# Attention, then two gated layers: in the third pair of heads, where six operand moves stand in the transfer queue

## The chip, the cores and the metric

The kernel runs on one core of a Trainium2 chip. The metric is the device time of one execution in microseconds (us); the time before is the median of three runs. The engines run side by side, each through its own queue in order: TensorE (PE; its weight loads are PEld), VectorE (DVE), ScalarE (ACT), GpSimd (POOL) and SyncE (SP), which issues the DMA transfers.

## The reference

```python
mask = q_assign[:, :, :, None] == k_assign[:, :, None, :]
scores = scale * np.matmul(q, k.transpose(0, 1, 3, 2))
scores = np.where(mask, scores, -1000000000.0)
attn = np.exp(scores - np.max(scores, axis=-1, keepdims=True))
attn = attn / (np.sum(attn, axis=-1, keepdims=True) + 1e-09)
out = np.matmul(attn, v)
...
h = (x @ w1) * (x @ w2) @ w3 @ w_out
gate = 1.0 / (1.0 + np.exp(-(h @ w_gate)))
y = (gate * (h @ w_val)) @ w_out2
```

Two batches of 8 heads, 768 tokens, 64 columns a head. A query sees only the keys whose nearest of 16 centroids is the same as its own. The attention output goes through the two layers of 512 to 1024 and 512 to 1536 columns.

## The kernel before

The attention stage takes the first 236 us or so. Two heads of 64 rows lie side by side on the 128 partitions as a pair; there are 8 pairs, numbered from 0, so the third pair is pair 2. A pair has six blocks of 256 queries, three for each head; the loop runs over blocks i, with `pr, at = divmod(i, 6)`. The order of all instructions is written out by hand, and each engine works through its own in that order.

Numbers are kept as a high part and a low part, and a product is made of parts. For a head four operand tiles are needed: QH and KH hold the high parts of q and k (64 rows) and below them 16 rows of the mask; QX and KX hold high and low parts (128 rows). `scores(j)` multiplies them into a score tile s (128 queries by 768 keys), DVE takes the maximum (L342), ACT the exponentials (L353), PE transposes them (L363, tile pt), ACT and DVE split them (tiles ph and pl, L381 and L392; in some blocks ACT copies to pc and POOL splits), and PE multiplies with v into av (L404, L405). ACT copies av to xa (L413), which frees the one av buffer for the next block.

While a pair is computed, the next pairs are made ready:
- `prep_split(later)` splits the raw q and k of the pair after the next into tiles hi and lo (L192 on ACT, L194 on DVE for q; L56 on ACT and L59 on POOL for k). It begins in block `at == 3`. Tiles hi and lo have two buffers each, one for q and one for k, so a pair's hi overwrites that of the pair before it.
- `prep_scatter(pr, e)` moves the rows of head e from hi and lo into its operand tiles: six transfers of 192 KB, four of high parts and two of low parts. `operands` has three buffers for each operand tile. For head 0 they stand at the end of the pair before (`at == 5`); for head 1 of pairs 3 to 7 in block `at == 1`.
- `prep_mask(pr, e)` moves the mask rows of a head (tile ohT, made by DVE in L273, half of it changed by POOL in L292) into QH and KH: four transfers of 24 KB. It stands in block `at == 3` for both heads.

For pair 2 alone, `prep_scatter(2, 1)` stands in block `at == 3` of pair 1, between the masks of the two heads. The same block issues, on ACT behind the exponentials, the first `prep_split` of pair 3 (L192).

All these transfers go through SP's queue, in order. When a transfer's source isn't made yet or its target is still read, SP waits and everything behind it waits too.

Of the kernel before, what the change touches and what calls it, by code (L numbers as in the profile page):

```python
# [27 lines left out]
def tile_cluster_attention__then__moe__then__gated_moe(  # L28
# [32 lines left out]
    def move(dst, src):  # L61
        nc.sync.dma_start(dst.bitcast(F32), src.bitcast(F32))
# [109 lines left out]
    def load_v(pr, e=None):  # L172
        if e != 1:
            raw[pr, "v"] = core.tile([128, 2, KT, D], F32, tag="vraw", name=f"vraw{pr}", bufs=1)
        which = slice(0, 2) if e is None else slice(e, e + 1)
        nc.sync.dma_start(raw[pr, "v"][:, which], v[pr][:, which])


    opnd = {}
# [33 lines left out]
    def operands(pr, e):  # L213
        opnd[pr, e] = tuple(core.tile([rows, S], F32R, tag=tag, name=f"{tag}{pr}_{e}", bufs=3) for tag, rows in (("QH", 96), ("KH", 96), ("QX", 128), ("KX", 128)))
        return opnd[pr, e]
# [2 lines left out]
        nc.vector.scalar_tensor_tensor(out=lo, in0=x, scalar=0.125, in1=hi.bitcast(F32), op0=ALU.mult, op1=ALU.subtract)  # L218

    def prep_scatter(pr, e):  # L220
        qh, ql, kh, kl = opnd[pr, "hl"]
        r = slice(64 * e, 64 * e + 64)
        QH, KH, QX, KX = operands(pr, e)
        move(QH[0:64], qh[r])
        move(KH[0:64], kh[r])
        move(QX[0:64], qh[r])
        move(KX[64:128], kh[r])
        move(KX[0:64], kl[r])
        move(QX[64:128], ql[r])

# [45 lines left out]
    def prep_mask(pr, e):  # L276
        ohT = opnd[pr, "oh"]
        QH, KH, _, _ = opnd[pr, e]
        halves = [slice(HALF * h, HALF * h + HALF) for h in range(2)]
        if pr == 0 and e == 0:  # L280
            for h in range(2):
                nc.vector.tensor_scalar(out=KH[64:96, halves[h]], in0=ohT[64 + 32 * h : 96 + 32 * h], scalar1=-1.0, scalar2=BIG, op0=ALU.add, op1=ALU.mult)
                nc.scalar.copy(QH[64:96, halves[h]], ohT[32 * h : 32 * h + 32])
            return
        if pr == 0:
            for h in range(2):
                nc.scalar.activation(KH[64:96, halves[h]], ohT[64 + 32 * h : 96 + 32 * h], AF.Copy, scale=BIG, bias=-BIG)
            nc.scalar.copy(QH[64:96, halves[0]], ohT[0:32])
            move(QH[64:96, halves[1]], ohT[32:64])
            return  # L290
        if e == 0:
            nc.gpsimd.tensor_scalar(out=ohT[64:128], in0=ohT[64:128], scalar1=-1.0, scalar2=BIG, op0=ALU.add, op1=ALU.mult)  # L292
        for h in range(2):
            at = 32 * h + C * e
            move(QH[64 : 64 + C, halves[h]], ohT[at : at + C])
            move(KH[64 : 64 + C, halves[h]], ohT[64 + at : 64 + at + C])
# [87 lines left out]
    def split_lo(i, k2):  # L384
        if (i, k2) not in pts:
            return
        src = pts.pop((i, k2))
        ph, pl = phs[i, k2]
        if by_pool(i, k2):
            split(src, ph, pl, nc.gpsimd, nc.gpsimd)  # L390
        else:
            nc.vector.tensor_tensor(out=pl, in0=src, in1=ph, op=ALU.subtract)  # L392
# [128 lines left out]
    hl = [core.tile([128, S], F32R, tag=tag, name=f"{tag}0_{w}", bufs=2) for w in range(2) for tag in ("hi", "lo")]  # L521
    opnd[0, "hl"] = hl
    QH, KH, QX, KX = operands(0, 0)
# [26 lines left out]
    scaled_lo(hl[1][up], q[up], hl[0][up])  # L550
    nc.gpsimd.tensor_tensor(out=hl[3][up], in0=k[up], in1=hl[2][up], op=ALU.subtract)
    prep_scatter(0, 1)
    load_v(0, 1)
    prep_v(0, 0)
# [15 lines left out]
    if True:  # L570
        for i in range(-2, NB + 2):
            pr, at = divmod(i, 6)
            nxt = pr + 1 if 0 <= i and pr + 1 < NPR else None
# [23 lines left out]
                join_x(pr - 1, 1)  # L597
            if nxt and nxt > 1 and at == 1:
                load_v(nxt)
                if nxt > 2:  # L600
                    prep_scatter(nxt, 1)
            if nxt and at == 3:
                for e in range(2):
                    if nxt == e == 1:
                        prep_scatter(1, 1)
                    prep_mask(nxt, e)
                    if nxt == 2 and e == 0:
                        prep_scatter(2, 1)
            split_lo(i - 1, 2)
            split_hi(i, 0)  # L610
            split_lo(i, 0)
# [190 lines left out]
    for n, (m, u) in enumerate(order):  # L802
# [6 lines left out]
        if n in W34_AT:  # L809
# [4 lines left out]
            for half in range(2):  # L814
                hl = wo_pool.tile([128, 2, HK, 128], F32R, tag="w3", name=f"w3_{j}_{half}", bufs=3)
# [437 lines left out]
```

## Time and profile before

| | us |
|---|---|
| median of 3 runs | 758.09 (757.73 to 758.61) |
| the profiled execution | 756.68 |
| its span in the trace | 754.7 |
| PE busy | 742.6 (98% of the span) |
| DVE busy | 575.6 (76%) |
| ACT busy | 473.5 (63%) |
| POOL busy | 414.7 (55%) |

The profiled execution took 1.98 us more than its span, and 1.41 us less than the median. Of the chain that ended last, 92% is work of PE. In the line of 40 slices PE is at 9 tenths or more nearly everywhere; the mean granted clock is 0.998 of full speed.

### The profile page before, as it was taken

How to read it: one execution, taken by the hardware profiler on the slowest of the kernel's cores; microseconds unless marked ns; L12 is line 12 of the kernel's file. 1: busy time of each engine (PE TensorE's matmuls, PEld its weight loads, DVE VectorE, ACT ScalarE, POOL GpSimd, SP SyncE). 2: the span in 40 equal slices, each digit the busy share in tenths (PEclk: the TensorE clock that was granted, in tenths of full speed). 3: DMA queues.
4: the chain of work that ended last, by engine and by line, in shares of the span. 5: the costliest groups of instructions: out<-in, count | busy, mean ns of one | idle time of the engine just before them, and what ended most of it. 6: DMA issues, size and time to landing. Idle time of an engine off the chain costs nothing.

```text
span 754.7 us, 12290 instructions
## 1 busy us (share of the span) xinstructions
PE 742.6 (98%) x4270; PEld 672.2 (89%) x4270; DVE 575.6 (76%) x893; ACT 473.5 (63%) x994; POOL 414.7 (55%) x420
## 2 busy tenths in 40 slices
PE   8997999999999999999999999999999999999998
PEld 7886988998998888888888999999999999999996
DVE  7996989999987777766753387686687978869675
ACT  8986888988886456555542355776756454565630
POOL 4776787888682665433231036675547646375510
PEclk9999999999999999999999999999999999999999
DMA  6675666785533444434340001221303113030004
GB/s 194 179 184 141 178 155 173 184 208 140 139 94 112 140 134 146 137 115 140 112 140 1 1 1 56 85 84 56 113 0 106 63 56 112 18 122 29 29 0 168
DMA packets 29054, 80.10 MB, mean 106 GB/s; under 512 B 5056, under 2 KB 6656, under 8 KB 28992
## 3 DMA queue, kind: packets, MB, share of 16 engines
q1 hardware_dynamic: 28992, 79.32, 36.0%
q8 instruction: 34, 0.56, 0.3%
q14 instruction: 28, 0.23, 0.1%
HBM read 52.46 MB, written 3.19 MB: 74 GB/s over the span
## 4 chain that ended last, share of the span: by engine, by line
PE 92%; DVE 2%; ACT 2%; DMA 1%; issue 1%; POOL 1%; SPq 0%; DVEq 0%; ACTq 0%; POOLq 0%
PE p L67 13%; PE p L66 13%; PE p L65 13%; PE s L330 8%; PE pt L363 7%; PE p_a L66 4%; PE p_a L67 4%; PE p_a L65 4%; PE av L404 4%; PE av L405 4%; PE p_b L65 2%; PE p_b L66 2%; PE p_b L67 2%; PE w34p L67 2%; PE w34p L66 2%; PE w34p L65 2%
## 5 line engine op out<-in xcount | busy, mean ns | idle before, releaser
L342 DVE TENSOR_REDUCE nm<-s 128x1 f32<-128x768 f32 x96 | 90.8, 947 | 7.9 <-PE s L330 6.6
L353 ACT ACTIVATE e<-s,nm 128x768 f32<-128x768 f32 x96 | 88.2, 919 | 13.1 <-DVE nm L342 12.6
L404 PE MATMUL av<-ph,vx 128*128 128x256 f32 x288 | 81.8, 310 | 5.0 <-ACT xa L413 4.7
L363 PE MATMUL pt<-ident,e 128*128 128x128 f32 x576 | 86.3, 273 | 0.2 <-DVE sm L246 0.2
L392 DVE TENSOR_TENSOR pl<-pt,ph 128x512 fp32r<-128x512 f32 x113 | 75.7, 682 | 10.9 <-ACT ph L381 9.7
L67 PE MATMUL p<-x,w 128*128 128x512 f32 (+1 forms) x208 | 80.2, 385 | 0.0
L66 PE MATMUL p<-x,w 128*128 128x512 f32 (+1 forms) x208 | 80.1, 385 | 0.0
L65 PE MATMUL p<-x,w 128*128 128x512 f32 (+1 forms) x208 | 80.1, 385 | 0.0
L405 PE MATMUL av<-pl,vx 128*128 128x256 f32 x288 | 75.6, 290 | 0.6 <-DMA raw<-in_qkT_dram 0.2
L116 POOL TENSOR_TENSOR w_a<-w_f 128x512 uint32<-128x512 uint32 x30 | 32.1, 1070 | 76.2 <-DVE w_f L115 36.1
L381 ACT CAST ph<-pt 128x512 fp32r<-128x512 f32 x113 | 64.7, 591 | 14.7 <-PE pt L363 13.4
L363 PEld LDWEIGHTS pt<-ident,e 128*128 128x128 f32 x576 | 68.1, 142 | 4.6 <-DVE sm L246 0.5
L1132 DVE TENSOR_TENSOR acc<-p,acc 128x512 f32<-128x512 f32 x59 | 40.5, 687 | 29.3 <-PE p L67 29.2
L948 POOL TENSOR_TENSOR wgv_a<-wgv_f 128x512 uint32<-128x512 uint32 x24 | 25.3, 1054 | 66.6 <-DVE wgv_f L947 38.3
L1026 ACT COPY s<-p_a 128x384 f32<-128x384 f32 x72 | 34.5, 479 | 43.1 <-PE p_a L67 42.8
L404 PEld LDWEIGHTS av<-ph,vx 128*128 128x128 f32 x288 | 54.9, 191 | 7.1 <-ACT xa L413 5.5
L405 PEld LDWEIGHTS av<-pl,vx 128*128 128x128 f32 x288 | 55.2, 192 | 3.3 <-DVE pl L392 3.2
L67 PE MATMUL p<-wo,u 128*128 128x512 f32 (+1 forms) x146 | 57.3, 393 | 0.0
L66 PE MATMUL p<-wo,u 128*128 128x512 f32 (+1 forms) x146 | 57.1, 391 | 0.0
L330 PE MATMUL s<-KH,QH 80*128 80x512 f32 x192 | 54.9, 368 | 1.7 <-ACT e L353 0.8
L65 PE MATMUL p<-wo,u 128*128 128x512 f32 (+1 forms) x146 | 56.3, 386 | 0.0
L330 PE MATMUL s<-KX,QX 128*128 128x512 f32 x192 | 49.9, 342 | 0.0
(254 smaller groups left out, 2222.9 us busy)
## 6 DMA issues: line engine op xcount, KB each, us to landing
wgv_f<-in_w_gv_dram SPq DMA_DIRECT2D x24, 512.0 KB, 3.3
wo_f<-in_w_out_dram SPq DMA_DIRECT2D x20, 512.0 KB, 3.2
w_f<-in_w_dram SPq DMA_DIRECT2D x16, 512.0 KB, 3.5
w_f<-in_w3T_dram SPq DMA_DIRECT2D x16, 512.0 KB, 3.3
raw<-in_qkT_dram SPq DMA_DIRECT2D x16, 384.0 KB, 4.7
r<-r_dram SPq DMA_DIRECT2D x16, 192.0 KB, 3.8
xb<-xa SPq DMA_DIRECT2D x15, 192.0 KB, 3.5
out_dram<-acc SPq DMA_DIRECT2D x11, 256.0 KB, 2.0
```

What stands on the lines that cost most here:

```text
L65: nc.tensor.matmul(ps, whi, xhi, start=start, stop=False, skip_group_check=more)
L66: nc.tensor.matmul(ps, whi, xlo, start=False, stop=False, skip_group_check=more)
L67: nc.tensor.matmul(ps, wlo, xhi, start=False, stop=stop, skip_group_check=more)
L330: nc.tensor.matmul(sp[:, c], products[n][0], products[n][1][:, c], start=n == 0, stop=n == 1)
L342: nc.vector.tensor_reduce(out=nms[j], in_=sps[j][:, 0:S], axis=AX.X, op=ALU.max, negate=True)
L353: nc.scalar.activation(et, sps.pop(j)[:, 0:S], AF.Exp, bias=nms.pop(j), accum_out=acc_x[pr, "sum"][:, at : at + 1])
L363: nc.tensor.transpose(pt[:, kk, 128 * t : 128 * t + 128], exps[2 * i + t][:, k0 : k0 + 128], ident)
L381: nc.scalar.copy(ph, pt)
L392: nc.vector.tensor_tensor(out=pl, in0=src, in1=ph, op=ALU.subtract)
L404: nc.tensor.matmul(avs[i], w, ph[:, kk, :], start=kt == 0, stop=False)
L405: nc.tensor.matmul(avs[i], w, pl[:, kk, :], start=False, stop=kt == KT - 1)
L1132: nc.vector.tensor_tensor(out=acc[:, t, :], in0=bk, in1=acc[:, t, :], op=ALU.add)
```

## The change

`prep_scatter` is divided into its four moves of high parts and its two moves of low parts. For the second head of pair 2, the four moves of high parts now stand in block `at == 1` of pair 1, directly behind the load of v. The two moves of low parts stay in block `at == 3`, between the masks of the two heads. Nothing is added or left out.

```diff
     def prep_scatter(pr, e):
+        prep_scatter_hi(pr, e)
+        prep_scatter_lo(pr, e)
+
+    def prep_scatter_hi(pr, e):
         qh, ql, kh, kl = opnd[pr, "hl"]
...
         move(KX[64:128], kh[r])
+
+    def prep_scatter_lo(pr, e):
+        qh, ql, kh, kl = opnd[pr, "hl"]
+        r = slice(64 * e, 64 * e + 64)
+        QH, KH, QX, KX = opnd[pr, e]
         move(KX[0:64], kl[r])
         move(QX[64:128], ql[r])
...
                 load_v(nxt)
+                prep_scatter_hi(nxt, 1)
                 if nxt > 2:
-                    prep_scatter(nxt, 1)
+                    prep_scatter_lo(nxt, 1)
...
                     if nxt == 2 and e == 0:
-                        prep_scatter(2, 1)
+                        prep_scatter_lo(2, 1)
```

The queue of SP in pair 1, from the load of v (vraw) on; QH_0 and KH_0 belong to the first head of pair 2, the names with _1 to its second head. Before:

```order
L176 DMA vraw_830<-in_v_dram 128x768
L62 DMA QH_0_690<-ohT_None 16x384
L62 DMA KH_0_691<-ohT_None 16x384
L62 DMA QH_0_690<-ohT_None 16x384
L62 DMA KH_0_691<-ohT_None 16x384
L62 DMA QH_1_969<-hi_0_546 64x768
L62 DMA KH_1_970<-hi_1_617 64x768
L62 DMA QX_1_971<-hi_0_546 64x768
L62 DMA KX_1_972<-hi_1_617 64x768
L62 DMA KX_1_972<-lo_1_618 64x768
L62 DMA QX_1_971<-lo_0_547 64x768
L62 DMA QH_1_969<-ohT_None 16x384
```

And in the changed kernel:

```order
L176 DMA vraw_830<-in_v_dram 128x768
L62 DMA QH_1_832<-hi_0_546 64x768
L62 DMA KH_1_833<-hi_1_617 64x768
L62 DMA QX_1_834<-hi_0_546 64x768
L62 DMA KX_1_835<-hi_1_617 64x768
L62 DMA QH_0_690<-ohT_None 16x384
L62 DMA KH_0_691<-ohT_None 16x384
L62 DMA QH_0_690<-ohT_None 16x384
L62 DMA KH_0_691<-ohT_None 16x384
L62 DMA KX_1_835<-lo_1_618 64x768
L62 DMA QX_1_834<-lo_0_547 64x768
L62 DMA QH_1_832<-ohT_None 16x384
```

The four moves out of hi have passed the four masks of the first head; the two moves out of lo have the masks ahead of them as before, and four transfers fewer between.

On ACT no row moved. This is its queue in block `at == 3` of pair 1 and the next, before and after alike but for line numbers: the split of pair 3 (hi_0_994), and what stands behind it.

```order
L353 ACTIVATE e_992,ss_656<-s_949,nm_962 128x768
L192 ACTIVATE hi_0_994<-raw_0_756 128x768
L381 CAST ph_1_1018<-pt_1_1013 128x512
L413 COPY xa_0_875<-av 128x256
L353 ACTIVATE e_1034,ss_656<-s_1005,nm_1031 128x768
L381 CAST ph_2_1041<-pt_2_1025 128x512
L378 COPY pc_1054<-pt_0_1044 128x512
```

The split stands ahead of the copy of av to xa and of the next exponentials.

## Rows read from the trace of the kernel before

**Rows 1.** PE's waits over the whole span: total us, times, longest.
```profile
PE av L404 <- ACT xa L413: 4.7, 1, 4.7
```

**Rows 2.** Timeline of ACT, pair 1: start, duration, instruction, [idle before, releaser].
```profile
59.49 0.91 ACT L353 ACTIVATE e<-s,nm 128x768 f32<-128x768 f32 x1
...
65.52 0.84 ACT L192 ACTIVATE hi<-raw 128x768 fp32r<-128x768 f32 x1 [5.04 <-DMA QX<-hi]
```

**Rows 3.** Timeline of PE, pair 1, same columns.
```profile
61.87 0.60 PE L363 MATMUL pt<-ident,e 128*128 128x128 f32 x4
67.16 0.49 PE L404 MATMUL av<-ph,vx 128*128 128x256 f32 x1 [4.69 <-ACT xa L413]
...
70.81 0.36 PE L404 MATMUL av<-ph,vx 128*128 128x256 f32 x1
...
75.58 0.27 PE L438 MATMUL s<-ident,ss 128*12 128x128 f32 x1
```

**Rows 4.** Windows: busy us by engine, then PEclk, DMA share and GB/s.
```profile
52.50:56.50 4.00, 4.00 (x31) 3.68 (x30) 3.90 (x7) 3.08 (x7) 3.74 (x5) 1.00 0.55 147
...
62.50:66.50 4.00, 0.00 (x0) 0.00 (x0) 0.00 (x0) 0.98 (x2) 0.00 (x0) 1.00 0.97 210
66.50:70.50 4.00, 3.34 (x14) 3.15 (x15) 3.55 (x5) 3.97 (x10) 1.37 (x2) 0.60 0.49 127
```

**Rows 5.** Timeline of SP's queue, pair 1: start and duration of each issue.
```profile
52.75 0.74 SPq L176 DMA_DIRECT2D vraw<-in_v_dram  x1
58.04 0.54 SPq L62 DMA_DIRECT2D QH<-ohT_None  x1
...
60.32 0.57 SPq L62 DMA_DIRECT2D KH<-ohT_None  x1
60.94 0.59 SPq L62 DMA_DIRECT2D QH<-hi  x1
...
62.27 0.53 SPq L62 DMA_DIRECT2D QX<-hi  x1
```

**Rows 6.** Timeline of ACT (first row) and PE at the same place of pair 2.
```profile
92.70 0.90 ACT L353 ACTIVATE e<-s,nm 128x768 f32<-128x768 f32 x1
...
95.10 0.60 PE L363 MATMUL pt<-ident,e 128*128 128x128 f32 x4
...
97.17 0.60 PE L330 MATMUL s<-KH,QH 80*128 80x512 f32 x2 [0.52 <-ACT pc L378]
...
98.31 0.36 PE L404 MATMUL av<-ph,vx 128*128 128x256 f32 x1
...
103.06 0.27 PE L438 MATMUL s<-ident,ss 128*12 128x128 f32 x1
```

**Rows 7.** Timeline of ACT and PE, the same place of pair 3, then pair 4.
```profile
120.18 0.90 ACT L353 ACTIVATE e<-s,nm 128x768 f32<-128x768 f32 x1
...
130.02 0.27 PE L438 MATMUL s<-ident,ss 128*12 128x128 f32 x1
...
146.13 0.90 ACT L353 ACTIVATE e<-s,nm 128x768 f32<-128x768 f32 x1
```

**Rows 8.** Timeline of PE and DVE, pair 1: last scores of head 0, the mask's tile.
```profile
50.48 0.52 PE L330 MATMUL s<-KX,QX 128*128 128x512 f32 x2
...
57.44 0.57 DVE L273 STREAM_TRANSPOSE ohT_None<-oh 128x384 f32<-128x384 f32 x1
```

**Rows 9.** Issue to landing of the moves to QX, of masks, of moves out of lo.
```profile
DMA to landing us min/median/max: 4.1/4.4/4.7
...
DMA to landing us min/median/max: 1.8/2.6/3.4
...
DMA to landing us min/median/max: 3.4/3.6/3.8
```

**Rows 10.** Timeline of DVE and POOL, pair 2.
```profile
97.19 1.35 DVE L194 SCALAR_TENSOR_TENSOR lo<-raw,hi 128x768 fp32r<-128x768 f32 x1
...
101.84 1.83 POOL L461 TENSOR_TENSOR xa<-xa,r 128x768 f32<-128x768 f32 x1 [0.35 <-DMA r<-r_dram]
```

## The prediction

> **What bounds the kernel now.** I read PE's waits first, since PE is busy for almost the whole span. The reader is to see that one wait stands far above the rest: PE waits 4.7 us, once, for ACT's copy of av to xa [rows 1]. So what PE can still win by a change of order lies in this one place, or in hidden places that the view doesn't name.
>
> Next I read the timelines around it. ACT ends its exponentials at 60.40 (59.49 + 0.91), and stands idle for 5.04 us, from 60.48 to 65.52, until a move QX<-hi lands; only then does it run L192, the split of pair 3's q into hi [rows 2]. L192 writes the buffer out of which that move reads pair 2's high parts, so it may not start earlier. Behind L192 in ACT's queue are the copy to xa and the next exponentials. PE has issued four transposes at 61.87 and can't go on before the copy has freed av: its next product starts at 67.16, after 4.69 us of idleness [rows 3]. Last I read why the move was late. SP issued the load of v at 52.75 and was then held until 58.04, by the mask (ohT) that DVE finished at 58.01 [rows 5, 8]. The four masks came next, and only then, from 60.94, the moves out of hi; QX<-hi was issued at 62.27 and landed at about 65.5 [rows 2, 5]. So four moves whose sources had long been made stood behind a wait that wasn't theirs.
>
> The stall has an aftermath. In the 4 us from 66.50 on the granted clock is 0.60 on the mean, against 1.00 in the windows before [rows 4]: PE worked part of that stretch at the lower of its two levels, 1.2 GHz.
>
> **What is moved, and when it lands.** The change moves four issues of SP and their four transfers; nothing else. They are now behind the load of v. Its issue ends at 53.49 (52.75 + 0.74), so the four go out from about 53.5; an issue costs 0.53 to 0.59 us and starts every 0.6 or so [rows 5], so the last ends near 56. What could hold them there? Their targets are the buffers of the first head of pair 1, whose last product on PE starts at 50.48 and takes 0.52 [rows 8]; their sources were read for the first head earlier. So I see no hold, and SP is through with them 2 us before the masks can go at 58.04: the masks are not issued later. QX<-hi is the third of the four, issued near 54.7. Before, it landed 3.25 us after its issue (62.27 to 65.52); moves to QX took up to 4.7 [rows 9]. So it lands between 58.0 and 59.4, and ACT wants it at 60.48: at least 1.1 us to spare. The DMA engines have the room, since in 52.50 to 56.50 they were busy 0.55 of the time [rows 4].
>
> **What the stall is worth.** I don't add 4.69 and an estimate of the clock; I compare with the next pair, which does the same work in this stretch with its moves issued early. Transposes to the first product of the next block but one: in pair 1 from 61.87 to 70.81, 8.94 us [rows 3]; in pair 2 from 95.10 to 98.31, 3.21 us [rows 6]. The difference is 5.73. A longer stretch gives the same: from the exponentials at 59.49 to the transpose of the sums at 75.58 pair 1 takes 16.09 [rows 2, 3], pair 2 from 92.70 to 103.06 takes 10.36 [rows 6], again 5.73. So nothing of the stall is made up by 75.58. Of it 4.69 is the idle wait, and the other 1.04 is what the low clock cost beyond pair 2's own small wait.
>
> That small wait is the open term. Pair 2 waits 0.52 us before the first scores of the next pair [rows 6]; the view names ACT's pc, but those scores also need the masks. Pair 3 does the same stretch in 9.84 (120.18 to 130.02) [rows 7], and so do two further pairs, in 9.88 and 9.84. Against them the gain is 16.09 - 9.84 = 6.25. With the changed order the last mask of the first head goes out at 60.32 as before and lands 1.8 to 3.4 later, 62.1 to 63.7 [rows 5, 9]. The scores want it at pair 2's time moved by the distance of the two pairs (92.70 - 59.49 = 33.21) and without its wait: 97.17 - 0.52 - 33.21 = 63.44. So the wait is between nothing and 0.3 by these rows, and 0.52 by pair 2. I take half of pair 2's: a gain of 6.25 - 0.25 = 6.0.
>
> On the transfer engines the masks follow the moves. The four are 768 KB, and at the 210 GB/s at which such moves went [rows 4] they need 3.7 us; started between 54.5 and 56 they end by 59.7, ahead of the last mask. The Trainium skill, in "DMA: Bandwidth & Descriptors", section on queues, rings and completion order, says that each DMA engine consumes a queue's descriptors in ring order, which speaks against putting large moves ahead of small urgent ones: by it the first mask would start up to 1.5 us later than before, the last one not at all, and the sum stays at 6.0.
>
> What is late next? **The low parts**: DVE's L194 writes a buffer out of which one of the two low moves reads. DVE wants it at 97.19 - 33.21 = 63.98 [rows 10]. The first low move goes out at 60.94, where QH<-hi went, and the second 0.6 later; by 3.4 to 3.8 of landing [rows 9] they are in at 64.3 to 64.7, or 65.0 to 65.4. So DVE may wait 0.3 to 1.4 us. Behind L194 on DVE stand the next maximum and so the exponentials; but PE has transposes and products queued. I cost this at nothing, since the row nearest to it is the lower bound, and PE has that much in hand; 1.4 stays for the range. **The sums r**: POOL wants them at about 101.49 - 33.21 = 68.3 [rows 10]; behind the low moves and four masks they go out near 65 and 65.6 and land some 3.6 later, as moves out of lo do [rows 9], at 69.2. POOL then waits some 0.9, against 0.35 in pair 2; I cost it at nothing, because POOL's work there is used by PE a block later, and 0.5 at most if that cover is gone.
>
> The sum: 754.7 - 6.0 = 748.7 us of span, with the 1.98 around it 750.7 for an execution like the profiled one. That one was 1.41 below the median, so against the median of the runs: 758.09 - 6.0 = **752.1 us**. About 0.2%, 1.5 us, is what a measurement of this kernel can tell from no change.
>
> **The rivals.**
> *The wait moves to the low parts or the masks.* For it speaks that only the high parts were moved, and that the pairs which lose nothing here issue all six moves early. Price: 1.4 us of DVE's wait fully on the path, and the full 0.52: 752.1 + 1.4 + 0.3 = 753.8; with a low move that lands after 4.7 like one to QX, 754.7. Against it: DVE's wait has to pass through exponentials and transposes before PE feels it.
> *The next pair goes better too.* From the transpose of the sums to the same exponentials of the next pair takes 17.12 in pair 3 (103.06 to 120.18) but 16.11 in pair 4 (130.02 to 146.13) [rows 6, 7]; pair 4 follows a pair that had no wait of 0.52. If pair 2 follows suit, 1.0 more is won: 751.1.
> *No effect.* L192 also waits for the raw q and for the moves of the first head; if one of these came at nearly the same time, the stall would stay: 758.1. Against it, they were issued in the pair before.
> *Slower.* The queue is in order and the four moves may have to wait at their new place. This decides if their target buffers are freed not by the scores that end at 51.0 but by the last scores of pair 1, which PE works just ahead of the transposes of 61.87 [rows 3]. Then the moves start at about 62.0, with the masks behind them; QX<-hi goes out at 63.2 and lands 3.25 to 4.7 later, at 66.5 to 67.9 instead of 65.52. The stall is 1.0 to 2.4 longer than before: 759.1 to 760.5. It costs time from a start of the four moves past 61.0 on, where QX<-hi comes to its old place. Against it stand the three buffers: in their turn those of the first head of pair 1 are next.
>
> **How the numbers follow.** The forecast (gain 5.4 to 6.6) has 0.63; the better next pair 0.12; the low parts or masks 0.17; no effect 0.05; slower 0.03. The range reaches from the better next pair with the whole 6.25, 758.09 - 7.3 = 750.8, to the high end of the first rival, 754.5; outside lie the last two cases and a little of the others, 0.14. Faster by over 0.2%: 0.92; within: 0.05; slower: 0.03, though the first half us of that rival would count as no change.
>
> **What would show it.** In the profile after: QX<-hi issued near 54.7; ACT's L192 at 60.5 with no idle time before it; PE's wait for xa gone from its list; the granted clock 1.00 from 62 to 72; the transpose of the sums near 69.5 instead of 75.58, and all later stages earlier by the same amount. Wrong would be: an idle time of ACT still before L192, SP held before the moves out of hi, a DVE wait of over 1 us before L194 with PE idle behind it, or a gain at 75 us that is lost again by 236 us.

## The result, and the profile after

| | before | after |
|---|---|---|
| median of 5 runs, us | 758.13 (757.73 to 758.71) | 751.46 (750.02 to 752.66) |
| the profiled execution, us | 756.68 | 751.46 |
| its span, us | 754.7 | 749.5 |

The ratio is 0.991 with a 95% interval of 0.9895 to 0.9926: a gain of 5.6 to 8.0 us, 6.7 between the medians. The prediction was 752.1, in a range of 750.8 to 754.5. Of 58 executions of the kernel before that were timed beside the experiments, 39 show a mean granted clock of 0.995 to 0.997 and took 758.5 us on the mean, and 19 show 0.998, as the profiled one does, and took 757.7; the changed kernel's five show 1.000. In the changed kernel the line numbers behind the new functions have grown by 9: L404 is now L413, L413 is L422, L438 is L447, L258 is L267, L461 is L470; the splits L192, L194 and L59 kept theirs.

PE's list of waits, over the whole span: total us, times, longest. It answers to [rows 1].

```profile
PE warm L137 <- POOL ident masks.py:199: 1.5, 1, 1.5
PE s L339 <- ACT e L362: 0.8, 1, 0.8
PE s L339 <- issue: 0.4, 1, 0.4
```

The wait of 4.7 us for xa is gone, and no new one has come. SP's queue in pair 1, from the load of v on, which answers to [rows 5]:

```profile
53.19 0.50 SPq L176 DMA_DIRECT2D vraw<-in_v_dram  x1
53.80 0.46 SPq L62 DMA_DIRECT2D QH<-hi  x1
...
55.43 0.47 SPq L62 DMA_DIRECT2D QX<-hi  x1
55.95 0.58 SPq L62 DMA_DIRECT2D KX<-hi  x1
58.13 0.54 SPq L62 DMA_DIRECT2D QH<-ohT_None  x1
...
59.99 0.59 SPq L62 DMA_DIRECT2D KH<-ohT_None  x1
60.62 0.59 SPq L62 DMA_DIRECT2D KX<-lo  x1
```

The four moves go out from 53.80 and QX<-hi at 55.43, 6.8 us earlier than before; the first mask goes out at 58.13 (58.04 before) and the last at 59.99 (60.32). ACT's timeline at the place of [rows 2]:

```profile
59.58 0.90 ACT L362 ACTIVATE e<-s,nm 128x768 f32<-128x768 f32 x1
60.47 0.84 ACT L192 ACTIVATE hi<-raw 128x768 fp32r<-128x768 f32 x1
...
61.67 0.38 ACT L422 COPY xa<-av 128x256 f32<-128x256 f32 x1
```

No bracket stands behind L192: the 5.04 us of idle time are gone, and the copy to xa begins at 61.67. PE's timeline and then its windows (busy us by engine, then granted clock, DMA share, GB/s), which answer to [rows 3, 4, 6]:

```profile
61.96 0.60 PE L372 MATMUL pt<-ident,e 128*128 128x128 f32 x4
...
63.34 0.51 PE L339 MATMUL s<-KH,QH 80*128 80x512 f32 x2
...
69.42 0.27 PE L447 MATMUL s<-ident,ss 128*12 128x128 f32 x1
```

```profile
62.50:66.50 4.00, 4.00 (x33) 3.77 (x31) 3.87 (x6) 3.97 (x11) 2.42 (x2) 1.00 0.50 131
66.50:70.50 4.00, 3.97 (x32) 2.94 (x31) 3.99 (x7) 3.10 (x8) 3.29 (x3) 1.00 0.96 226
```

From the exponentials at 59.58 to the transpose of the sums at 69.42 it now takes 9.84 us, against 16.09 before [rows 2, 3]: 6.25 are won here. The clock stays at 1.00 where it had been 0.60. The scores at 63.34 wait for no mask. The span, though, became only 5.2 shorter. The transposes of the sums show where the missing 1.0 went: from pair 3's to pair 4's took 25.99 before (130.02 to 156.01) and takes 26.97 after (123.79 to 150.76), while the other intervals behind pair 1 differ by less than 0.1. Two rows of PE after, then one before (pair 3's stands in [rows 7]):

```profile
123.79 0.27 PE L447 MATMUL s<-ident,ss 128*12 128x128 f32 x1
150.76 0.27 PE L447 MATMUL s<-ident,ss 128*12 128x128 f32 x1
```

```profile
156.01 0.27 PE L438 MATMUL s<-ident,ss 128*12 128x128 f32 x1
```

The experiments with the argmax, below, tell why.

### The profile page after: what moved, and what is told of

The parts are those of the page before. It is cut to its first block, busy times and chain, and to the rows that moved or that the text cites. A ratio compares the mean times of both kernels' runs of the same rounds, so it can differ in the third digit from the quotient of the medians.

```text
span 749.5 us, 12291 instructions
## 1 busy us (share of the span) xinstructions
PE 742.0 (99%) x4270; PEld 670.9 (90%) x4270; DVE 575.9 (77%) x893; ACT 473.5 (63%) x994; POOL 415.2 (55%) x420
## 4 chain that ended last, share of the span: by engine, by line
PE 91%; DVE 3%; DMA 3%; ACT 1%; issue 1%; POOL 0%; SPq 0%; DVEq 0%; ACTq 0%; POOLq 0%
PE p L67 13%; PE p L66 13%; PE p L65 13%; PE s L339 7%; PE pt L372 6%; PE p_a L66 4%; PE p_a L65 4%; PE p_a L67 4%; PE av L414 4%; PE av L413 4%; PE p_b L65 2%; PE p_b L66 2%; PE p_b L67 2%; PE w34p L66 2%; PE w34p L65 2%; PE w34p L67 2%
## 5 line engine op out<-in xcount | busy, mean ns | idle before, releaser
L413 PE MATMUL av<-ph,vx 128*128 128x256 f32 x288 | 81.3, 308 | 0.4 <-POOL pl L59 0.2
L413 PEld LDWEIGHTS av<-ph,vx 128*128 128x128 f32 x288 | 54.4, 189 | 2.7 <-POOL pl L59 1.5
```

Of the source, the lines that this page charges most:

```text
L413: nc.tensor.matmul(avs[i], w, ph[:, kk, :], start=kt == 0, stop=False)
```

## The experiments

Each kernel was timed against the kernel before on the same chip, whose median there was 758.2 to 758.4. The expectations are those written before each run.

**The changed kernel again** (a1_after_again), nothing edited.

> The changed kernel again, on the chip of the next two runs. It lay between 750.0 and 752.7; I expect the same, in steps of about 1.0 us. Theory on the spread: in block at == 1 of each pair DVE's comparison L267 (two tiles in) meets POOL's subtraction L59 (two tiles in); the one that starts second is held until the other ends. Where DVE comes second, L267 takes 1.59 instead of 0.56 us and the pair is 1.0 us longer. So the number of long L267 in the profile goes with the time. Rival: the spread has to do with transfers, and L267 is as often long in fast as in slow executions.

Measured: 751.48 (750.87 to 751.95, 4 runs), ratio 0.9906 [0.9886, 0.9927]. The result repeats. In its profiled execution (751.93) all five comparisons are of the long kind (1.57 to 1.59), and there is no trace of a faster one, so the theory on the spread isn't tested by it.

**Two of the four moves early: q's, or k's** (e1_q_early, e2_k_early). In e1 only QH and QX go early and KH and KX follow behind the two low moves; in e2 it is the other way round, and QH and QX stand behind the first head's masks, as before. Two small functions hold the two moves that go first (`scatter_first`) and the two others (`scatter_rest`); the diff is the call.

```diff
-                prep_scatter_hi(nxt, 1)
+                (prep_scatter_hi if nxt > 2 else scatter_first)(nxt, 1)
...
+                        scatter_rest(2, 1)
```

> The changed kernel, but of the four moves of high parts only the two that read q's tile (QH, QX) stand early; the two of k's tile come last, behind the two low moves. My theory: the gain is ACT's L192 no longer waiting for QX<-hi, and L192 waits for q's tile alone. So L192 starts at about 60.5 with no idle time, PE's wait of 4.7 us for xa is gone, and the time is 751 to 754; ACT's L56 (k's high part), wanted at 65.0, waits up to 1.4 us for the late KX<-hi. Rival, the gain comes from fewer bytes in the queue at that place: half of the four moves are still there, so half the gain, about 755.

> The converse: only the two moves of k's tile stand early, the two of q's tile stay behind the first head's masks. My theory: QX<-hi goes out at about 61.3 instead of 62.3 and lands near 64.5, so L192 still waits, some 4.0 instead of 5.0 us; PE still has its wait for xa, 3.7 instead of 4.7; the time is 756.5 to 757.5. Rival, bytes in the queue: half the gain, about 755.

Measured: e1 752.52 (751.62 to 752.87), ratio 0.9926 [0.9908, 0.9943], as expected. e2 753.36 (753.00 to 753.62), ratio 0.9938 [0.9922, 0.9955], three us under the lower end of what was expected. The rival of half the gain, about 755, was met by neither. ACT's timeline tells why; first e1, then e2 with SP's issue of QX<-hi:

```profile
60.29 0.84 ACT L192 ACTIVATE hi<-raw 128x768 fp32r<-128x768 f32 x1
66.36 0.83 ACT L56 CAST hi<-raw 128x768 fp32r<-128x768 f32 x1 [1.50 <-DMA KH<-ohT_None]
```

```profile
60.74 0.84 ACT L192 ACTIVATE hi<-raw 128x768 fp32r<-128x768 f32 x1
...
61.54 0.59 SPq L62 DMA_DIRECT2D QX<-hi  x1
```

In e2, L192 ran at 60.74 with no idle time, although QX<-hi, which reads q's old hi, was issued only at 61.54, after L192 had started. So L192 isn't bound to q's buffer. What fits e1 and e2 alike is that the two buffers of hi form one pool: the next split takes the one whose readers stand first in the program, and the other is left to the split of k (L56), which comes some 4.5 us later. The traces don't name the buffers, so this rule is inferred. In e1 this is L56's turn to wait: 1.50, and PE's 1.6 for xa behind it. The view names a mask as its releaser; I take it to be KX<-hi, issued close by, since that is what reads the buffer. e2 lost its 1.9 us against the changed kernel elsewhere: DVE's L194 waited 1.1 for KX<-lo, POOL 2.4 for r, and the transpose of the sums came at 70.74. Of these waits PE felt the first, through DVE's low part:

```profile
65.51 1.57 DVE L194 SCALAR_TENSOR_TENSOR lo<-raw,hi 128x768 fp32r<-128x768 f32 x1 [1.09 <-DMA KX<-lo]
68.60 0.39 PE L428 MATMUL av<-pl,vx 128*128 128x256 f32 x1 [0.79 <-DVE pl L415]
```

**Nothing moved, but no buffer to wait for** (e3a_hi_elsewhere, e3b_hi_lo_elsewhere). The order is that of the kernel before. In e3a pair 2's hi tiles lie in tiles of x that are free then, so the next split overwrites nothing that a late move reads; in e3b its lo tiles do too (the diff is e3b's; e3a has only the lines on hi).

```diff
-            hi = core.tile([128, S], F32R, tag="hi", name=f"hi{pr}_{w}", bufs=2)
-            lo = core.tile([128, S], F32R, tag="lo", name=f"lo{pr}_{w}", bufs=2)
+            hi = spare(0, w) if pr == 2 else core.tile([128, S], F32R, tag="hi", name=f"hi{pr}_{w}", bufs=2)
+            lo = spare(1, w) if pr == 2 else core.tile([128, S], F32R, tag="lo", name=f"lo{pr}_{w}", bufs=2)
```

> The kernel before, with all moves at their old places, but pair 2's high parts are made in other buffers, so that pair 3's split overwrites nothing that the late moves still read. My theory: the idle time of ACT before L192 is gone although no move is earlier. But the low parts, which share their two buffers as before, are now late: KX<-lo goes out at 63.5 and lands near 67.1, DVE wants L194 at 64.0, so DVE waits about 3 us there and PE behind it; and r, issued at 68.6, is late for POOL by some 3 us. A gain of 2 to 3 us, 755 to 756. Rival, the order of the queue in itself is what was won: no gain, 758, whatever buffers are used.

> As the one before, and pair 2's low parts in other buffers too. My theory: neither ACT's L192 nor DVE's L194 waits, with every move at its old place. What stays is r, issued at 68.6, landing near 72.2, which POOL wants at 68.3: POOL waits 3 to 4 us, and the split that PE reads a block later is up to 2.3 us late. The time is 752 to 755; the difference to the run before is the price of late low parts. Rival, the order of the queue: 758.

Measured: e3a 756.25 (755.26 to 757.83), ratio 0.9975 [0.9965, 0.9985], just above the 755 to 756 expected. e3b 759.00 (757.81 to 759.70), ratio 1.0012 [1.0002, 1.0021], no gain where 752 to 755 was expected. In both, L192 runs at 60.3 to 60.4 without idle time, with QX<-hi as late as before (its source is now a tile of x). Rows of ACT and of SP's queue in e3a:

```profile
60.43 0.84 ACT L192 ACTIVATE hi<-raw 128x768 fp32r<-128x768 f32 x1
62.40 0.53 SPq L62 DMA_DIRECT2D QX<-x  x1
```

So the buffer of hi is what held ACT: shown. What comes next is the interesting part. In e3a DVE's L194 waits for the low move, and PE behind it; these are a row of DVE's waits, one of PE's timeline and a window:

```profile
DVE lo L194 <- DMA KX<-lo: 3.5, 1, 3.5
```

```profile
70.06 0.39 PE L405 MATMUL av<-pl,vx 128*128 128x256 f32 x1 [2.61 <-DVE pl L392]
```

```profile
70.50:74.50 4.00, 4.00 (x22) 3.00 (x21) 3.36 (x6) 2.09 (x5) 1.43 (x2) 0.62 0.97 231
```

Of 3.5 us of waiting at DVE 2.61 reach PE, and the granted clock falls to 0.62 in the window behind. In e3b this wait is gone too, and the transpose of the sums stands at 69.19, all of the gain; then the sums r, last in the queue (issued at 68.61), hold POOL and through it PE:

```profile
74.44 1.83 POOL L461 TENSOR_TENSOR xa<-xa,r 128x768 f32<-128x768 f32 x1 [6.26 <-DMA r<-r_dram]
...
80.02 0.38 PE L404 MATMUL av<-ph,vx 128*128 128x256 f32 x1 [3.90 <-POOL ph L54]
81.37 0.58 PE L405 MATMUL av<-pl,vx 128*128 128x256 f32 x1 [0.96 <-POOL pl L59]
```

PE is idle for 4.86 us in all, some 14 us behind the wait that had been cured, and the low clock follows:

```profile
82.50:86.50 4.00, 4.00 (x19) 3.81 (x19) 1.36 (x2) 1.17 (x4) 3.22 (x4) 0.50 0.87 218
```

The next transpose of the sums comes at 104.17, after 34.98 us where the kernel before takes 27.48: 7.5 are lost for the 6.4 won. The rival's time (758) is met, but not by its mechanism, since neither split waits. The mechanism was foreseen, its price was not: r landed 5.1 us after its issue, not some 3.6, and POOL waited 6.26 instead of 3 to 4.

**Late moves, with r ahead of them** (e7_late_moves_r_first). This is e3b, and POOL's addition of xb and the load of r behind it stand ahead of the six moves. This asks if lateness itself costs anything once nobody waits there.

```diff
+                        add_x(pr - 1)
+                        spread(pr - 1, "xb", 1)
                         prep_scatter(2, 1)
...
-            if 0 < pr and i < NB and at == 3:
+            if 0 < pr and i < NB and at == 3 and nxt != 2:
```

> The kernel before, all six moves at their old place; tiles hi and lo of pair 2 lie in other buffers, so nothing that is split next waits for a move; and the transfer of the sums r is issued ahead of the six moves in place of behind them. Nothing of the result changes. Theory (the moves' lateness costs only through the three things that wait for something in the queue: the split of q, the low part of q, the sums): no idle time before L192, before L194 or of POOL for r over 1 us, transpose of the sums at 69 to 70, time 750 to 753, as the changed kernel though the moves go out 6 us later. Rival (late moves cost in themselves, by the masks or operands behind them): PE waits over 2 us before the first scores of pair 2 or later, time 755 to 759.

Measured: 756.48 (755.02 to 757.78, 12 runs), ratio 0.9973 [0.9964, 0.9983]. My theory's time is missed, the rival's is met, though not at its place. L192 (60.25), L194 (63.84) and POOL's multiplication by r (L461, 68.10) all start without a wait, and the transpose of the sums stands at 69.15. The loss comes one pair later, as these rows of ACT and PE show:

```profile
90.57 0.84 ACT L192 ACTIVATE hi<-raw 128x768 fp32r<-128x768 f32 x1 [3.31 <-issue]
...
92.22 0.39 PE L404 MATMUL av<-ph,vx 128*128 128x256 f32 x1 [2.97 <-ACT xa L413]
```

It is the old stall again. The late moves kept SP's queue busy, so pair 3's moves for its first head went out from 70.84 (65.77 in the changed kernel), the move of xa at 82.09 (77.64), and pair 3's QX<-hi for its second head at 84.47 (80.02). That one landed 6.0 us later, at 90.5, just when L192 starts. So a queue that was 5.1 us late at one pair's end was still 4.4 late in the next, where something waited for it.

**All six moves early** (e4_all_six_early). The two low moves go early too.

```diff
                 prep_scatter_hi(nxt, 1)
-                if nxt > 2:
-                    prep_scatter_lo(nxt, 1)
+                prep_scatter_lo(nxt, 1)
```

> The changed kernel with the two low moves early as well, as pairs 3 to 7 have it. By my theory the low moves cost nothing where they are (DVE's L194 started at 64.06 without idle time), so nothing is won: the same as the changed kernel within 1 us, 750 to 753. Rival, that the low parts still hold something back: 0.5 to 1.4 us faster than the changed kernel.

Measured: 751.93 (751.49 to 752.93), ratio 0.9917 [0.9899, 0.9934]; the changed kernel on the same chip had 751.48. The difference is too small to tell, and the rival's 0.5 to 1.4 us are not won. The profiled execution shows one thing that the changed kernel's doesn't: the first mask goes out at 58.95, the last at 61.49, and the scores wait for it.

```profile
64.73 0.59 PE L339 MATMUL s<-KH,QH 80*128 80x512 f32 x2 [0.89 <-DMA KH<-ohT_None]
```

**The microsecond that was lost again: the argmax** (e5_argmax_later, e6_pool_later, e6_again, e8_pool_later_12). In the interval of 25.99 before, and in none of after, DVE's comparison in the argmax is short. Rows of DVE and POOL in pair 4, first of before, then of after:

```profile
138.60 0.56 DVE L258 TENSOR_TENSOR sm<-sm,mx_None 128x384 f32<-128x384 f32 x1
138.72 1.59 POOL L59 TENSOR_TENSOR pl<-pc,ph 128x512 fp32r<-128x512 f32 x1
```

```profile
132.35 1.59 DVE L267 TENSOR_TENSOR sm<-sm,mx_None 128x384 f32<-128x384 f32 x1
132.25 1.28 POOL L59 TENSOR_TENSOR pl<-pc,ph 128x512 fp32r<-128x512 f32 x1
```

Both instructions read two tensors from SBUF. The one that starts 0.1 us earlier keeps its time (0.56, or 1.28), and the other is longer by 1.03 or 0.31. How long it is held follows from the other's end: in every such meeting in the traces of before, of after and of e1 to e4 and e7, the held comparison ends 0.40 to 0.43 us behind POOL's subtraction, whether it began 0.02 or 0.7 us after it (1.67 long at 77.99 and 1.00 at 51.60 of after), and a held subtraction ends 1.13 to 1.15 behind the comparison. Before, four of the five comparisons of pairs 2 to 6 were of the long kind (1.57 to 1.59), after, all five (1.59 to 1.67). The Trainium skill, in "SBUF — State Buffer", section "Who interferes with whom", says that a DVE instruction with two SBUF inputs contends with a GpSimd instruction that reads SBUF, but not with one that only writes it, and that the one that issues first makes the other wait. These rows agree on who waits; the held one ends some 0.14 us earlier than if all of it came behind the other's end. Two ways to change who is first were tried, both on the changed kernel: e5 moves the argmax behind the block's last split; e6 puts six small memsets of POOL between its high part and its subtraction (e8: twelve), so that POOL comes second.

```diff
-            split(src, ph, pl, nc.gpsimd, nc.gpsimd)
+            nc.gpsimd.tensor_scalar(out=ph, in0=src, scalar1=1.0, scalar2=1.0, op0=ALU.mult, op1=ALU.mult)
+            if i % 6 == 1 and 2 <= i // 6 < END:
+                for _ in range(6):
+                    nc.gpsimd.memset(pad_t, 0.0)
+            nc.gpsimd.tensor_tensor(out=pl, in0=src, in1=ph, op=ALU.subtract)
```

> The changed kernel with the maximum and the comparison over the centroids (L266, L267), and POOL's product after them, behind the block's last split instead of behind its first. Same work, other place in DVE's queue. Theory: DVE then makes the next scores' maximum 1.1 to 2.1 us earlier, L267 no longer meets POOL's L59 and takes about 0.56 us; up to 1.0 us is won in each of the five pairs where it took 1.59: 746 to 748, and less spread. Rival: PE doesn't wait for DVE there, or the meeting moves to another pair of instructions: 751, as the changed kernel.

> The changed kernel with six small memsets of POOL between its copy of the high part and its subtraction of it, in the second block of pairs 2 to 6, so that DVE's comparison of the maxima (L267 of the changed kernel) starts before POOL's subtraction in place of behind it. Nothing of the result changes. Theory (the two instructions hold each other up; the second to start waits for the first, and it matters which): DVE's comparison takes 0.56 in all five pairs in place of 1.59, POOL's subtraction some 1.6 in place of 1.28, each of the five intervals between transposes of sums falls by about 1.0 (26.97 to 25.99), time 746 to 748. Rival (the interval of 25.99 had another cause, or POOL's later low part is what PE waits for): the comparison is short, but the time is 751 or more.

> The kernel with six memsets once more, for a second profiled execution: the first took 746.47 but the median was 748.60. If the order of DVE's comparison and POOL's subtraction is not the same in every execution, an execution some 2 us longer shows one or two comparisons of about 1.6 in place of 0.56, and the intervals between transposes of sums are longer by 1.0 in just those pairs. Rival: all five are 0.56 and the difference lies elsewhere.

> The same with twelve memsets in place of six, so that POOL's subtraction begins another 1.0 us later. Nothing of the result changes. Theory (with six, POOL is still first in some executions): with twelve DVE is first in more of them, the median falls from 748.6 to 746 to 747.5 and the runs spread less. Rival (the rest of the spread has another cause, or the low part now comes late for PE): median 748.5 or more, and in the latter case PE waits for POOL's low part.

Measured: e5 757.37 (756.83 to 758.65), ratio 0.9990 [0.9981, 0.9999]: the gain of the change is lost. The 746 to 748 of the theory and the 751 of the rival are both missed, though the meeting moved as the rival had it. The comparison is 0.56 in all five pairs, but the argmax's next instruction with two inputs now starts behind POOL's subtraction and is long instead, and PE waits for DVE's low parts. Rows of DVE, POOL and PE's waits:

```profile
142.31 1.50 DVE L278 TENSOR_TENSOR oh<-sm,mc_None 128x384 f32<-128x384 f32 x1
142.11 1.29 POOL L59 TENSOR_TENSOR pl<-pc,ph 128x512 fp32r<-128x512 f32 x1
```

```profile
PE av L414 <- DVE pl L401: 8.3, 9, 1.1
```

e6: 748.60 (746.47 to 749.26), ratio 0.9873 [0.9857, 0.9888]; again: 748.19 (747.79 to 748.97), ratio 0.9871 [0.9856, 0.9885]. That is 3 us less than the changed kernel, and its profiled execution of 746.47 has a span of 744.7. Rows of DVE and POOL in pair 4:

```profile
129.98 0.56 DVE L268 TENSOR_TENSOR sm<-sm,mx_None 128x384 f32<-128x384 f32 x1
129.72 1.00 POOL L403 MEMSET pad<- 128x24 f32 x6
130.68 1.29 POOL L404 TENSOR_TENSOR pl<-pc,ph 128x512 fp32r<-128x512 f32 x1
```

The comparison is 0.56 in all five pairs, beside memsets of 0.12 that read nothing. POOL's subtraction stays at 1.29, not at 1.6 as I had expected, since the comparison is over before it starts. The intervals between transposes of sums are 26.20, 25.93 and 25.98 (69.29, 95.49, 121.42, 147.40) against 27.41, 26.96 and 26.97; the last two pairs win 0.7 each. So the theory holds and gives 0.7 to 1.2 us a pair in this execution; of the 746 to 748 expected, the medians stay 0.2 to 0.6 short. In the second profiled execution (span 746.5) all five comparisons were 0.56 too, so the rest of the spread isn't theirs, as the rival had it: its intervals from 95.51 are 26.85 and 26.55, with two waits that the first didn't have (0.64 at 116.46 and 0.33 at 143.00), in PE's list:

```profile
PE s L340 <- DMA KH<-ohT_None: 1.0, 2, 0.6
```

With the pairs shorter the masks are next. e8: 750.85 (750.23 to 751.05), ratio 0.9902 [0.9885, 0.9918]: its theory is missed. Twelve memsets give most of it back, though its comparisons are short (0.56 to 0.60); PE waits for POOL's low part once in each of the five pairs:

```profile
PE av L419 <- POOL pl L404: 2.7, 5, 0.8
```

A short comparison isn't always worth 1.0 us. In e7 and e3a, where one comparison came first (135.06 and 190.88), its interval was shorter by 0.45 and 0.7; in e2 the one at 79.30 met nothing, but the argmax's next instruction with two inputs was then held (83.79, 1.54 us), and the interval was 27.24 against 27.41 of the changed kernel.

## Why the prediction was right, point by point

**What bounded.** Right: the one large wait was the stall, and its way (QX<-hi late, ACT's L192, the copy to xa, PE) is shown by the profile after and by e3a and e3b, which take the wait at L192 away without touching the order. One link was told wrongly: that L192 writes the buffer out of which QX<-hi reads. e2 ran L192 before QX<-hi was even issued. What L192 needs, as e1 and e2 together suggest, is the first of two buffers to come free by the order of the program; the four moves together free both. The description of the kernel before has the same error, with one buffer for q and one for k. And e3a and e3b show what the prediction's chain of waits leaves out: with the wait at L192 gone by itself only 1.9 us are won, and with that at L194 gone too nothing, because the low parts, and then r, in the same late queue, come due. The change wins because it makes the queue early enough for all three.

**When the moves go.** Right: from 53.80 (53.5 foreseen), QX<-hi at 55.43 instead of 54.7, masks not later, L192 at 60.47 (60.48). When QX<-hi landed no row shows, since nothing waited for it. The rival in which the moves are held at their new place didn't occur, nor the one without effect.

**What the stall is worth.** 6.25 by pair 3's row; 6.25 measured. I had taken 0.25 off for a wait for the masks, and there was none at 63.34. It was a fair risk: with all six moves early it was 0.89.

**What is late next.** Costed at nothing, and nothing it was. L194 started at 64.06 with no wait (0.3 to 1.4 feared); POOL waited 0.70 for r (0.9 foreseen, 0.35 in pair 2), and PE felt nothing. Rows of DVE and POOL after:

```profile
64.06 1.36 DVE L194 SCALAR_TENSOR_TENSOR lo<-raw,hi 128x768 fp32r<-128x768 f32 x1
69.08 1.83 POOL L470 TENSOR_TENSOR xa<-xa,r 128x768 f32<-128x768 f32 x1 [0.70 <-DMA r<-r_dram]
```

The reason given for the low parts, that PE has that much work in hand, is not borne out: in e2 a wait of 1.09 at L194 left PE idle for 0.79. That the low parts cost nothing was because the wait didn't come, not because of the cover: KX<-lo went out at 60.62, 0.3 us earlier than reckoned, and with the shortest landing of 3.4 us [rows 9] it was in at about 64.0 (an estimate), just when L194 began. Here the prediction had luck. The margin is small, as e3a and e3b show too: 3.5 us late at L194 cost PE 2.61 and a stretch at the low clock, 6.26 us at POOL cost 4.86 and another.

**The size.** The profiled gain was 5.2 in span, for a sum of 6.0; between medians 6.7. Against the sum made on one profiled execution stands the comparison of 0.56 in that execution, 1.0 us that the profile after hadn't. Without it the span fell by 6.2. The kernel before was profiled in one of its better executions: one comparison was short, and the granted clock of 0.998 was above that of most. The prediction carried the 1.41 us between that execution and the median over to the changed kernel, whose profiled execution is itself the median. So three errors lie in the sum, 0.25 too much for the masks, 1.41 that didn't carry over and 0.98 left out for the comparison, and in part they cancel: 752.1 - 0.25 - 1.41 + 0.98 = 751.4, with 751.46 measured. That the number came within 0.7 owes something to luck, the size of the stall doesn't. No trace of the kernel before in a slower execution shows what its 1.41 is made of. The range's upper end is said to be that of the first rival, which the prediction itself puts at 754.7, not 754.5; nothing hangs on it.

**The rival "the next pair goes better"** was argued from 17.12 against 16.11 [rows 6, 7], and that argument falls: the 1.01 between them is the short comparison at 138.60 (1.59 - 0.56 = 1.03), and has nothing to do with the wait of 0.52 in the pair ahead. Pair 2 went no better after the change (27.41 against 27.48). The same place, read rightly, was worth 3 us more (e6).

**What stays open.** How often the comparison is short in other executions of the kernel before can't be read from its one profile. In the changed kernel and its repeat all five were long, in executions of 751.46 and 751.93; the fastest (750.02) has no trace, so whether the comparison spreads its runs over 750.0 to 752.7 stays open. In e6 and e6_again all were short and the spans still lay 1.8 apart; the landing of the masks is a candidate, not shown. In e2 the waits at L194 and for r weren't tried apart.

## What to carry to other kernels

In a queue that works in order, a transfer whose source is ready should not stand behind one whose source isn't; but read first what will be late next, and price it, since of three things that waited on this queue, freeing one or two gained little or nothing (e3a, e3b), and a queue left late presented the same bill a pair later (e7). To estimate such a stall, compare the stretch with the same stretch of a pair that has none: it included the clock's part without an estimate. And where two profiled stretches of equal work differ by a round amount, compare the durations of single instructions ahead of looking for a wait: none of the lists of waits here shows an instruction that is held inside its own span.

## What was not expected of the hardware

DVE's comparison with two SBUF inputs (128 x 384) takes 0.56 us alone and 1.57 to 1.67 when POOL's subtraction (two SBUF inputs, 1.28) began 0.02 to 0.13 us earlier; when DVE was 0.02 to 0.20 earlier, POOL's took 1.51 to 1.67. The held instruction ends at a fixed distance behind the other's end (0.40 to 0.43 us for DVE's, 1.13 to 1.15 for POOL's). Such a meeting cost the pair up to 1.0 us (0.98 in pair 4 of before against after; 0.45 and 0.7 in e7 and e3a), and a tenth of a microsecond decided it. That a pair can pay the full 1.0 fits with how full DVE is there: it was busy 3.93 of the 4 us from 78.50 to 82.50 of the changed kernel.
